# A Fourier mixing and squared-ReLU kernel: another order of its first phase and first block

## The chip, the cores and the metric

The kernel runs on one core of a Trainium2 chip. The metric is the device time of one execution in microseconds (us). The kernel before the change ran four times: 1963.38, 1964.35, 1965.85 and 1966.34 us, median 1965.1 us.

Its engines are named as in the profile: PE (TensorE, matrix products; PEld are its weight loads), DVE (VectorE), ACT (ScalarE), POOL (GpSimd) and SP (SyncE, which issues most DMAs; SPq is its queue).

## The reference

```python
def _attn_ref(x):                       # x: (8, 3008, 256)
    X = np.fft.fft(x, axis=1)
    X = np.fft.fft(X, axis=2)
    return X.real.astype(np.float32)
...
def _moe_ref(x, w_in, w_out):           # x: (24064, 256); w_in: (256, 2048); w_out: (2048, 256)
    h = x @ w_in
    r = np.maximum(h, 0.0)
    g = r * r
    return (g @ w_out).astype(np.float32)
```

The second function takes the first one's output, with batch and sequence as one axis. Everything is float32 in the kernel; the two weights arrive as float64 and are converted on the chip.

## The kernel before, in words

**Transform.** The real part of the transform over the sequence needs, for each of the 8 batches, three tables by frequency: Pt (cosine rows), Qt (sine rows) and Et (one middle column). The kernel halves the sequence again and again by symmetry. `fold(b, t)` (L340) folds one of 7 tiles of rows: three DVE steps for the P part (`f_s`, `f_sc`, `f_w`) and three for the Q part (`f_d`, `f_dc`, `f_w`). Tiles 0 to 3 are the even rows, tiles 4 to 6 the odd ones. `dft_ops(b)` (L435) gives the products: for each of P, E, Q and for even and odd frequencies (kp) a group of five operations: `even_n` (PE products over tiles 0 to 3, with cosT or sinT, and one ACT copy), `join_4` and `join_2` (DVE sums and differences), `odd_n` (PE products over tiles 4 to 6) and `join_1` (DVE, writes Pt, Et or Qt). For batch 0 the groups are numbered from 0: P 0 to 4 and 5 to 9, E 10 to 14 and 15 to 19, Q 20 to 24 and 25 to 29; number 0, 5, 10, ... is `even_n`, and so on in the order named.

**Weights.** The transform over the last axis is multiplied into w_in beforehand. `load_win(j)` (L253) loads and converts one 256-column pair of w_in (`convert`, L213: two DMAs, two DVE and three ACT operations at once; three DVE operations, L244, L246 and L247, in its `finish`); its `products` (L258) form G1 and G2 by four PE products (tile pg, L262), copied by ACT (L263), and gE by four products with a moving operand of one column (tile pe, L268) and an ACT operation. `load_wout(j)` converts one pair of w_out. Both kinds take 8 rounds (j = 0 to 7).

**Main loop.** A step (L767) is one pair j of 128-wide feature tiles for one block of 251 columns. There are 8 steps in a block, 6 blocks in a batch, 384 steps in all. `front` (L541) makes four PE products (tile ph: L551 with G1 and Pt, L552 with G2 and Qt) and six DVE operations (L554, L556, L557, twice); `combine` (L564) is ReLU and square on ACT and, outside the first block, four POOL operations; `back` (L582), two steps later (LAG = 2), adds up the output products in PSUM: eight PE products (L591) in the first block, seven (L604) afterwards, for which `sum_wout` (L278) forms sums of weights in the second block. `gather` and `store` end a block. Every float32 product is two records on PE (768 calls of L551 are 1536 records).

**Order.** The program sets the order on each engine by hand. Lines 711 to 747 write out the first phase for batch 0. The weights are a list (L683) that `next_weight` (L689) works off, up to two in a step of the first block; each call starts the next conversion and then finishes the one begun. While a batch is in the main loop, the folds and transforms of the next batch (`ahead`, L672) are let in between the halves of `front` by `between` (L754): each piece has a cost, and a pace spreads the sum over the steps. It lets in nothing in the first block, half the pace in the second, and the full pace after it.

**PSUM.** Three pools share the eight banks: psh (tag h, two buffers: ph, and pg), psd (tag d, two buffers: the transform's pd, and pe) and psm (mA, mB, mC, mD, one each; the plain `back` of the first block writes mA and mB alone).

Of the kernel before, what the change touches and what calls it, by code (L numbers as in the profile page):

```python
# [8 lines left out]
F32 = mybir.dt.float32  # L9
# [4 lines left out]
P = 128  # L14
# [67 lines left out]
def kernel(  # L82
# [12 lines left out]
    nc = tc.nc  # L95
# [7 lines left out]
    NJ = NFC // 2  # L103
# [56 lines left out]
    cosd = const.tile([P, 2, P], F32, name="cosd")  # L160
    sind = const.tile([P, 2, P - 1], F32, name="sind")
    altd = const.tile([P, 2, 1], F32, name="altd")
    cosT = const.tile([P, 2, WT], F32, name="cosT")
# [4 lines left out]
    G1 = const.tile([P, F], F32, name="G1")  # L168
    G2 = const.tile([P - 1, F], F32, name="G2")
    gE = const.tile([P, NFC], F32, name="gE")  # L170
# [17 lines left out]
    nc.vector.memset(ramp[:, 1:2], 255.0 * 2.0 ** 23)  # L188
    for dst, src in ((cosd, cos_d), (sind, sin_d), (altd, alt_d)):
        nc.scalar.dma_start(out=dst, in_=src.rearrange("(c p) m -> p c m", p=P))  # L190


# [60 lines left out]
    def load_win(j):  # L253

        w = ep.tile([P, 2, CH], F32, name="win", tag="sB" if j % 2 else "sA")
        finish = convert(parts(w, 1), pair_in(j))

        def products():  # L258
            for tab, G, n in ((cosd, G1, P), (sind, G2, P - 1)):
                ps = psh.tile([P, CH], F32, name="pg", tag="h")  # L260
                for i in range(2):
                    nc.tensor.matmul(ps[0:n], tab[:, i], w[:, i], start=i == 0, stop=i == 1)  # L262
                nc.scalar.copy(G.rearrange("p (h j f) -> j p h f", h=2, j=NJ)[j],  # L263
                               ps[0:n].rearrange("p (h f) -> p h f", h=2))
            ps = psd.tile([P, CH], F32, name="pe", tag="d")
            for h in range(2):
                for i in range(2):
                    nc.tensor.matmul(ps[:, h:h + 1], w[:, i, h * P:(h + 1) * P], altd[:, i],  # L268
                                     start=i == 0, stop=i == 1)
            nc.scalar.mul(gE[:, j::NJ], ps[:, 0:2], 0.5)  # L270

        return finish, products

    def load_wout(j):

        return convert(wout[:, j].rearrange("p h c e -> p h (c e)"), pair_out(j)), lambda: None

# [157 lines left out]
    def dft_ops(b):  # L435
# [7 lines left out]
        def group(kp, which):  # L443
# [40 lines left out]
            def odd_n():  # L484
                ps = psd.tile([P, 512], F32, name="pd", tag="d")[0:n]
                st["odd"] = ps[:, 0:n0]
# [54 lines left out]
    def front(b, k0, n, j, between):  # L541

        pt, qt, et = PQE[b]
        ks = slice(k0, k0 + n)
        g = gp.tile([P, 2, 2, CK], F32, name="g", tag="g")
        for h in range(2):
            fc = j + NJ * h
            fs = slice(fc * P, (fc + 1) * P)
            ps = psh.tile([P, 2, CH], F32, name="ph", tag="h")
            hP, hQ = ps[:, 0, 0:n], ps[:, 1, 0:n]  # L550
            nc.tensor.matmul(hP, G1[:, fs], pt[:, ks], start=True, stop=True)  # L551
            nc.tensor.matmul(hQ, G2[:, fs], qt[:, ks], start=True, stop=True)  # L552
            t = hp.tile([P, CK], F32, name="he", tag="he")[:, 0:n]
            nc.vector.scalar_tensor_tensor(out=t, in0=et[:, ks], scalar=gE[:, fc:fc + 1], in1=hP,  # L554
                                           op0=ALU.mult, op1=ALU.add)
            tt(out=g[:, h, 0, 0:n], in0=t, in1=hQ, op=ALU.add)  # L556
            tt(out=g[:, h, 1, 0:n][:, ::-1], in0=t, in1=hQ, op=ALU.subtract)  # L557
            between()
        return g
# [22 lines left out]
    def back(n, j, g, s, final):  # L582

        if j == 0:
            for nm in ("mA", "mB", "mC", "mD"):
                acc[nm] = psm.tile([P, 2, CH], F32, name=nm, tag=nm)
# [20 lines left out]
    def gather(n, plain, final):  # L607


        mA, mB, mC, mD = (acc[nm] for nm in ("mA", "mB", "mC", "mD"))  # L610
        if plain:
            c = ep.tile([P, 2, 2, CK], F32, name="c", tag="c")
            for side, m in enumerate((mA, mB)):
                nc.scalar.copy(c[:, side, :, 0:n], m[:, :, 0:n])
            return c
        sA = ep.tile([P, 2, CK], F32, name="sA", tag="sA")
        sB = ep.tile([P, 2, CK], F32, name="sB", tag="sB")
# [63 lines left out]


    weights = [lambda j=j: load_win(j) for j in range(2)]  # L683
    for j in range(NJ):
        weights.append(lambda j=j: load_wout(j))
        if j + 2 < NJ:
            weights.append(lambda j=j: load_win(j + 2))

    def next_weight():  # L689

        nonlocal begun
        (finish, products), begun = begun, weights.pop(0)() if weights else None
        finish()
        return products

    pieces = [fold(0, t) for t in range(NT)]
# [13 lines left out]

    begun = weights.pop(0)()
    for t in range(NT):
        load_x(0, t)
    load_table(cosT, cos_s, nc.sync)
    load_table(sinT, sin_s, nc.sync)
    start()
    for_p(0)
    finish, products = begun
    finish()
    products()  # L720
    for t in range(1, 4):
        for_p(t)
    groups_at(0, 5)
    for_p(4)
    for_q(0)
    for_q(1)
    groups_at(1, 2)
    for_p(5)
    groups_at(6, 7)
    for_p(6)  # L730
    groups_at(3)
    for_q(4)
    groups_at(4, 8)
    for_q(5)
    groups_at(9, 10)
    for_q(6)
    groups_at(11, 12, 13)
    begun = weights.pop(0)()
    groups_at(15)
    for_q(2)  # L740
    groups_at(14, 16, 17, 18)
    for_q(3)
    groups_at(20, 19, 25)
    products = [next_weight()]
    groups_at(21, 22, 23, 26, 27, 28)
    next_weight()
    groups_at(24, 29)
    LAG = 2
# [5 lines left out]
    def between():  # L754


        nonlocal spent
        if i < NJ or i % NJ == LAG - 1:
            return
        spent -= pace / 2 if i < 2 * NJ else pace  # L760
        while side and spent <= 0:
            t, f = side.pop(0)
            f()
            spent += t

    flight, finished = [], []
    for i in range(len(steps) + LAG + 4):  # L767
        if i < len(steps):
# [8 lines left out]
            if i % per == 0:  # L777
                assert not side
                side = ahead(b + 1) if b + 1 < B else []
                calls = 2 * (NJ - 1) * len(BLOCKS) - 6  # L780
                spent, pace = 0.0, sum(t for t, _ in side) / (calls - (0 if i else 3 * (NJ - 1)))
            g = front(b, k0, n, j, between)
            if i < NJ:
                s = combine(n, g, True)
            elif i < 2 * NJ:
                sum_wout(j)
        while finished and finished[0][0] <= i:
            store(*finished.pop(0)[1:])
        if i >= LAG and flight:
# [3 lines left out]
            if at[3] == NJ - 1:  # L793
                c_ = gather(at[2], s_ is None, final)
                finished += [(i + 2 + s, *at[:3], s, c_, final) for s in range(2)]
        for f in products:
            f()
        products = [next_weight() for _ in range(2 if 0 < i < NJ - 2 else 1 if i < NJ else 0)]
        if i < len(steps):
# [64 lines left out]
```

## Time and profile before

| what | value |
|---|---|
| runs | 1963.38, 1964.35, 1965.85, 1966.34 us; median 1965.1 |
| profiled execution, its own time | 1963.38 us |
| its span in the profile | 1961.6 us, 27513 instructions |
| PE busy | 1924.4 us (98%) |
| DVE busy | 1399.1 us (71%) |
| ACT busy | 924.8 us (47%) |
| POOL busy | 1168.8 us (60%) |
| HBM read, written | 42.39 MB, 24.68 MB |

All times in the profile count from the start of the span, so 1.8 us of the execution lie outside it. A line of the timeline gives start, duration, engine, line of the code, operation, tiles (output, then inputs), shape and count (x4: four records merged), and in brackets how long the engine had been idle and who released it. A line of the waits gives the waiting engine and line, what it waited for, the sum in us, the number of times and the longest. The duration of a matmul record runs to its modelled end and overlaps the next one; the spacing of starts is the rate. PEclk is the TensorE clock that was granted, 1.00 being full.

### The profile page before, as it was taken

The numbers are of one execution on the slowest core, as the hardware profiler recorded it, in microseconds if no ns is written. First come the engines' busy times: TensorE is split into PE (matmuls) and PEld (weight loads), VectorE is DVE, ScalarE is ACT, GpSimd is POOL, SyncE is SP. The second block draws the span as 40 slices with busy tenths as digits, with TensorE's granted clock in tenths as the row PEclk, the third lists the DMA queues.
The fourth block names the chain that finished last, engine by engine and source line by source line (L and its number), as shares of the span: only waits on it lengthen the run. The fifth ranks groups of instructions, "written<-read, shape, count | busy, mean of one in ns | idle before, by whom it ended". The sixth has DMA issues, their size and how long they took to land.

```text
span 1961.6 us, 27513 instructions
## 1 busy us (share of the span) xinstructions
PE 1924.4 (98%) x9160; PEld 1705.2 (87%) x9160; DVE 1399.1 (71%) x3434; ACT 924.8 (47%) x1076; POOL 1168.8 (60%) x1705
## 2 busy tenths in 40 slices
PE   5999999999999999999999999999999999999998
PEld 3788888888988889888998889888898888988887
DVE  7888867777677776777668776677767777655554
ACT  1654544455444444444444454444544454444443
POOL 0037745667466755666556765666756676556564
PEclk8999999999999999999999999999999999999999
DMA  6332101211021111111011200121002101100101
GB/s 189 116 44 53 27 13 40 49 27 23 13 51 41 23 26 27 41 33 35 12 35 35 46 20 12 36 52 27 20 16 52 33 11 22 27 11 11 22 11 22
DMA packets 145340, 68.88 MB, mean 35 GB/s; under 512 B 129003, under 2 KB 136110, under 8 KB 145197
## 3 DMA queue, kind: packets, MB, share of 16 engines
q1 hardware_dynamic: 144121, 66.60, 15.8%
q8 instruction: 72, 1.18, 0.3%
q10 hardware_dynamic: 1076, 0.52, 0.1%
q14 instruction: 71, 0.58, 0.1%
HBM read 42.39 MB, written 24.68 MB: 34 GB/s over the span
## 4 chain that ended last, share of the span: by engine, by line
PE 93%; DVE 4%; ACT 1%; DMA 1%; issue 0%; SPq 0%; DVEq 0%; ACTq 0%
PE ph L552 16%; PE ph L551 16%; PE mC L604 16%; PE mA L604 16%; PE mB L604 16%; PE mD L604 8%; PE pd L455 2%; PE pd L500 2%; DVE he L554 1%; DVE g L557 0%; DMA cosT<-in_cos_s_dram 0%; DVE g L556 0%; ACT g L566 0%; ACT g L567 0%; DMA xt<-in_x_dram 0%
## 5 line engine op out<-in xcount | busy, mean ns | idle before, releaser
L566 ACT ACTIVATE g<-g 128x1004 f32<-128x1004 f32 (+1 forms) x384 | 399.5, 1040 | 817.3 <-DVE g L557 439.3
L574 POOL TENSOR_TENSOR s<-g 128x251 f32<-128x251 f32 (+1 forms) x376 | 245.6, 653 | 717.6 <-ACT g L567 655.8
L554 DVE SCALAR_TENSOR_TENSOR he<-Et,gE,ph 128x251 f32<-128x251 f32 (+1 forms) x768 | 361.9, 471 | 421.9 <-PE ph L552 420.8
L551 PE MATMUL ph<-Pt,G 128*128 128x251 f32 (+1 forms) x1536 | 451.8, 375 | 4.2 <-ACT G L263 3.4
L552 PE MATMUL ph<-Qt,G 127*128 127x251 f32 (+1 forms) x1536 | 451.4, 374 | 0.4 <-DVE Qt L468 0.4
L567 ACT ACTIVATE g<-g 128x1004 f32<-128x1004 f32 (+1 forms) x384 | 399.2, 1040 | 12.1
L604 PE MATMUL mC<-s,wsum 128*128 128x251 f32 (+1 forms) x1504 | 381.4, 374 | 0.0
L604 PE MATMUL mA<-g,wout 128*128 128x251 f32 (+1 forms) x1504 | 379.8, 374 | 0.0
L556 DVE TENSOR_TENSOR g<-he,ph 128x251 f32<-128x251 f32 (+1 forms) x768 | 320.5, 417 | 54.3 <-POOL s L574 0.5
L551 PEld LDWEIGHTS ph<-Pt,G 128*128 128x128 f32 x1536 | 287.3, 189 | 42.1 <-ACT G L263 4.0
L552 PEld LDWEIGHTS ph<-Qt,G 127*128 127x128 f32 x1536 | 291.2, 190 | 36.6 <-DVE Qt L468 0.8
L604 PEld LDWEIGHTS mC<-s,wsum 128*128 128x128 f32 x1504 | 285.5, 190 | 34.6
L557 DVE TENSOR_TENSOR g<-he,ph 128x251 f32<-128x251 f32 (+1 forms) x768 | 314.4, 409 | 0.0
L604 PEld LDWEIGHTS mA<-g,wout 128*128 128x128 f32 x1504 | 282.8, 189 | 34.7 <-issue 0.6
L575 POOL TENSOR_TENSOR s<-s,g 128x251 f32<-128x251 f32 (+1 forms) x376 | 282.9, 753 | 29.5
L576 POOL TENSOR_TENSOR s<-g 128x251 f32<-128x251 f32 (+1 forms) x376 | 294.9, 784 | 0.0
L577 POOL TENSOR_TENSOR s<-g,s 128x251 f32<-128x251 f32 (+1 forms) x376 | 254.7, 677 | 0.0
L604 PE MATMUL mB<-g,wsum 128*128 128x251 f32 (+1 forms) x752 | 220.5, 374 | 0.0
L604 PE MATMUL mD<-s,wout 128*128 128x251 f32 (+1 forms) x752 | 220.3, 374 | 0.0
L604 PE MATMUL mB<-s,wout 128*128 128x251 f32 (+1 forms) x752 | 219.9, 374 | 0.0
L604 PEld LDWEIGHTS mB<-g,wsum 128*128 128x128 f32 x752 | 142.6, 190 | 17.4
L604 PEld LDWEIGHTS mD<-s,wout 128*128 128x128 f32 x752 | 141.9, 189 | 17.7
(118 smaller groups left out, 1283.0 us busy)
## 6 DMA issues: line engine op xcount, KB each, us to landing
out_dram<-os SPq DMA_DIRECT2D x376, 56.0 KB
xt<-in_x_dram SPq DMA_DIRECT2D x32, 384.0 KB
xt<-in_x_dram SPq DMA_DIRECT2D x42, 128.0 KB
Et<-e_dram SPq DMA_DIRECT2D x7, 752.5 KB
xt<-in_x_dram SPq DMA_DIRECT2D x9, 512.0 KB
out_dram<-os SPq DMA_DIRECT2D x288, 6.8 KB
raw<-in_moe_w_in_dram SPq DMA_DIRECT2D x16, 256.0 KB
raw<-in_moe_w_out_dram SPq DMA_DIRECT2D x16, 256.0 KB
```

The lines of the kernel that those rows point to most:

```text
L551: nc.tensor.matmul(hP, G1[:, fs], pt[:, ks], start=True, stop=True)
L552: nc.tensor.matmul(hQ, G2[:, fs], qt[:, ks], start=True, stop=True)
L554: nc.vector.scalar_tensor_tensor(out=t, in0=et[:, ks], scalar=gE[:, fc:fc + 1], in1=hP, op0=ALU.mult, op1=ALU.add)
L556: tt(out=g[:, h, 0, 0:n], in0=t, in1=hQ, op=ALU.add)
L557: tt(out=g[:, h, 1, 0:n][:, ::-1], in0=t, in1=hQ, op=ALU.subtract)
L566: act(v, v, AF.Relu)
L567: act(v, v, AF.Square)
L574: gt(out=s1, in0=g21, in1=g22, op=ALU.add)
L575: gt(out=s2, in0=s1, in1=g11, op=ALU.subtract)
L576: gt(out=s3, in0=g11, in1=g21, op=ALU.subtract)
L577: gt(out=s4, in0=g12, in1=s2, op=ALU.subtract)
L604: nc.tensor.matmul(acc[nm][:, i, 0:n], w, v[:, 0:n], start=j == 0 and i == 0, stop=j == NJ - 1, skip_group_check=True)
```

## The change

The first x tiles are loaded ahead of the first weights. The first phase has a new order: the P parts of all tiles come ahead of the first join, the Q parts of the odd rows (tiles 4 to 6) ahead of those of tiles 1 to 3. `odd_n` of batch 0 takes its PSUM buffer from psh in place of psd. `awake(n)` issues n float32 products of the 128x128 identity with itself into a tile that nothing reads; 96 stand ahead of everything else on PE, 20 more behind the first weight products. The alternating column altd becomes column 127 of the sine table, so that G2 has 128 rows, the last of which holds what pe held; `for_e` takes it out with two one-column products and a DVE multiplication in place of four products and an ACT operation. pg takes mC and mD in place of psh. The weights have an order of their own (`weights`, `leftover`): in each step of the first block, behind `front`, the products of the pair j = i + 1, the start of one w_out, the finish of the w_in of i + 2, the start of that of i + 3; behind `back`, the finish of w_out and `for_e`. Before the main loop no w_out is converted. `between` lets in nothing in the second block, and the pace is the sum over the steps that are left.

```diff
@@ -158,15 +158,14 @@
         nc.sync.dma_start(out=xt[b, t][0:rows], in_=x[b, r0:r0 + step * (rows - 1) + 1:step])
     cosd = const.tile([P, 2, P], F32, name="cosd")
-    sind = const.tile([P, 2, P - 1], F32, name="sind")
-    altd = const.tile([P, 2, 1], F32, name="altd")
+    sind = const.tile([P, 2, P], F32, name="sind")
     cosT = const.tile([P, 2, WT], F32, name="cosT")
     sinT = const.tile([P, 2, WT], F32, name="sinT")
     wout = const.tile([P, NJ, 2, 2, H], F32, name="wout")
     wsum = const.tile([P, 3, NJ, H], F32, name="wsum")
     ident = const.tile([P, P], F32, name="ident")
     G1 = const.tile([P, F], F32, name="G1")
-    G2 = const.tile([P - 1, F], F32, name="G2")
+    G2 = const.tile([P, F], F32, name="G2")
     gE = const.tile([P, NFC], F32, name="gE")
     def load_table(tab, src, engine):
@@ -186,8 +185,15 @@
     ramp = const.tile([P, 2], F32, name="ramp")
     nc.vector.memset(ramp[:, 0:1], 1151.0)
     nc.vector.memset(ramp[:, 1:2], 255.0 * 2.0 ** 23)
-    for dst, src in ((cosd, cos_d), (sind, sin_d), (altd, alt_d)):
+    for dst, src in ((cosd, cos_d), (sind[:, :, 0:P - 1], sin_d), (sind[:, :, P - 1:], alt_d)):
         nc.scalar.dma_start(out=dst, in_=src.rearrange("(c p) m -> p c m", p=P))
+    filled = psm.tile([P, CH], F32, name="filled", tag="mB")
+    def awake(n):
+        for _ in range(n):
+            nc.tensor.matmul(filled[:, 0:P], ident, ident, start=True, stop=True)
     def pair_in(j):
@@ -256,24 +262,27 @@
         finish = convert(parts(w, 1), pair_in(j))
         def products():
-            for tab, G, n in ((cosd, G1, P), (sind, G2, P - 1)):
-                ps = psh.tile([P, CH], F32, name="pg", tag="h")
+            for tab, G, nm in ((cosd, G1, "mC"), (sind, G2, "mD")):
+                pg = psm.tile([P, CH], F32, name="pg", tag=nm)
                 for i in range(2):
-                    nc.tensor.matmul(ps[0:n], tab[:, i], w[:, i], start=i == 0, stop=i == 1)
+                    nc.tensor.matmul(pg, tab[:, i], w[:, i], start=i == 0, stop=i == 1)
                 nc.scalar.copy(G.rearrange("p (h j f) -> j p h f", h=2, j=NJ)[j],
-                               ps[0:n].rearrange("p (h f) -> p h f", h=2))
+                               pg.rearrange("p (h f) -> p h f", h=2))
+        def for_e():
             ps = psd.tile([P, CH], F32, name="pe", tag="d")
             for h in range(2):
-                for i in range(2):
-                    nc.tensor.matmul(ps[:, h:h + 1], w[:, i, h * P:(h + 1) * P], altd[:, i],
-                                     start=i == 0, stop=i == 1)
-            nc.scalar.mul(gE[:, j::NJ], ps[:, 0:2], 0.5)
-        return finish, products
+                fc = j + NJ * h
+                nc.tensor.matmul(ps[:, h:h + 1], G2[:, fc * P:(fc + 1) * P], ident[:, P - 1:], start=True, stop=True)
+            return lambda: nc.vector.tensor_scalar_mul(gE[:, j::NJ], ps[:, 0:2], 0.5)
+        return finish, products, for_e
     def load_wout(j):
-        return convert(wout[:, j].rearrange("p h c e -> p h (c e)"), pair_out(j)), lambda: None
+        return convert(wout[:, j].rearrange("p h c e -> p h (c e)"), pair_out(j))
     def sum_wout(j):
@@ -482,7 +491,9 @@
                 both(st["c"][:, 0:n1], st["c"][:, n1:n0], a, ps[:, 2 * n2:2 * n2 + n1])
             def odd_n():
-                ps = psd.tile([P, 512], F32, name="pd", tag="d")[0:n]
+                pool, tag = (psh, "h") if b == 0 else (psd, "d")
+                ps = pool.tile([P, 512], F32, name="pd", tag=tag)[0:n]
                 st["odd"] = ps[:, 0:n0]
                 if not b:
                     return product(ps[:, 0:n0], 3)
@@ -549,7 +560,7 @@
             ps = psh.tile([P, 2, CH], F32, name="ph", tag="h")
             hP, hQ = ps[:, 0, 0:n], ps[:, 1, 0:n]
             nc.tensor.matmul(hP, G1[:, fs], pt[:, ks], start=True, stop=True)
-            nc.tensor.matmul(hQ, G2[:, fs], qt[:, ks], start=True, stop=True)
+            nc.tensor.matmul(hQ, G2[0:P - 1, fs], qt[:, ks], start=True, stop=True)
             t = hp.tile([P, CK], F32, name="he", tag="he")[:, 0:n]
             nc.vector.scalar_tensor_tensor(out=t, in0=et[:, ks], scalar=gE[:, fc:fc + 1], in1=hP,
                                            op0=ALU.mult, op1=ALU.add)
@@ -582,7 +593,7 @@
     def back(n, j, g, s, final):
         if j == 0:
-            for nm in ("mA", "mB", "mC", "mD"):
+            for nm in ("mA", "mB") if s is None else ("mA", "mB", "mC", "mD"):
                 acc[nm] = psm.tile([P, 2, CH], F32, name=nm, tag=nm)
         if s is None:
             for c in range(2):
@@ -607,12 +618,13 @@
     def gather(n, plain, final):
-        mA, mB, mC, mD = (acc[nm] for nm in ("mA", "mB", "mC", "mD"))
+        mA, mB = acc["mA"], acc["mB"]
         if plain:
             c = ep.tile([P, 2, 2, CK], F32, name="c", tag="c")
             for side, m in enumerate((mA, mB)):
                 nc.scalar.copy(c[:, side, :, 0:n], m[:, :, 0:n])
             return c
+        mC, mD = acc["mC"], acc["mD"]
         sA = ep.tile([P, 2, CK], F32, name="sA", tag="sA")
         sB = ep.tile([P, 2, CK], F32, name="sB", tag="sB")
         u = ep.tile([P, 3, CK], F32, name="u", tag="u")
@@ -680,19 +692,6 @@
                 + groups + [(0.0, lambda: load_e(1))])
-    weights = [lambda j=j: load_win(j) for j in range(2)]
-    for j in range(NJ):
-        weights.append(lambda j=j: load_wout(j))
-        if j + 2 < NJ:
-            weights.append(lambda j=j: load_win(j + 2))
-    def next_weight():
-        nonlocal begun
-        (finish, products), begun = begun, weights.pop(0)() if weights else None
-        finish()
-        return products
     pieces = [fold(0, t) for t in range(NT)]
     start, *groups = [f for _, f in dft_ops(0)]
@@ -708,43 +707,50 @@
         for i in which:
             groups[i]()
-    begun = weights.pop(0)()
-    for t in range(NT):
+    def rounded(j):
+        win[j][0]()
+    start()
+    awake(96)
+    load_x(0, 0)
+    load_x(0, 1)
+    for_p(0)
+    for_q(0)
+    for_p(1)
+    win = [load_win(0)]
+    for t in range(2, NT):
         load_x(0, t)
     load_table(cosT, cos_s, nc.sync)
     load_table(sinT, sin_s, nc.sync)
-    start()
-    for_p(0)
-    finish, products = begun
-    finish()
-    products()
-    for t in range(1, 4):
-        for_p(t)
+    for_p(2)
+    rounded(0)
+    win[0][1]()
+    awake(20)
+    for_p(3)
     groups_at(0, 5)
     for_p(4)
-    for_q(0)
+    for_p(5)
+    for_p(6)
+    groups_at(3, 8, 1, 2)
+    for_q(4)
+    groups_at(6, 7)
+    for_q(5)
+    groups_at(10, 15, 4)
+    for_q(6)
+    groups_at(9, 13, 18, 11, 12, 16, 17)
     for_q(1)
-    groups_at(1, 2)
-    for_p(5)
-    groups_at(6, 7)
-    for_p(6)
-    groups_at(3)
-    for_q(4)
-    groups_at(4, 8)
-    for_q(5)
-    groups_at(9, 10)
-    for_q(6)
-    groups_at(11, 12, 13)
-    begun = weights.pop(0)()
-    groups_at(15)
+    groups_at(14, 23)
+    win.append(load_win(1))
+    groups_at(19, 28)
+    copy_e = win[0][2]()
     for_q(2)
-    groups_at(14, 16, 17, 18)
     for_q(3)
-    groups_at(20, 19, 25)
-    products = [next_weight()]
-    groups_at(21, 22, 23, 26, 27, 28)
-    next_weight()
-    groups_at(24, 29)
+    groups_at(20, 25)
+    copy_e()
+    win.append(load_win(2))
+    rounded(1)
+    groups_at(21, 22, 24, 26, 27, 29)
     LAG = 2
     BLOCKS = [(k0, min(CK, NKT - k0)) for k0 in range(0, NKT, CK)]
     steps = [(b, k0, n, j) for b in range(B) for k0, n in BLOCKS for j in range(NJ)]
@@ -755,13 +761,34 @@
         nonlocal spent
-        if i < NJ or i % NJ == LAG - 1:
+        if i < 2 * NJ or i % NJ == LAG - 1:
             return
-        spent -= pace / 2 if i < 2 * NJ else pace
+        spent -= pace
         while side and spent <= 0:
             t, f = side.pop(0)
             f()
             spent += t
+    late = []
+    def weights():
+        if i + 1 < NJ:
+            win[i + 1][1]()
+        now = i - 1 if i < NJ - 1 else i
+        if now >= 0:
+            late.append(load_wout(now))
+        if i + 2 < NJ:
+            rounded(i + 2)
+        if i + 3 < NJ:
+            win.append(load_win(i + 3))
+        elif i == NJ - 2:
+            late.append(load_wout(i))
+    def leftover():
+        while late:
+            late.pop(0)()
     flight, finished = [], []
     for i in range(len(steps) + LAG + 4):
@@ -777,12 +804,14 @@
             if i % per == 0:
                 assert not side
                 side = ahead(b + 1) if b + 1 < B else []
-                calls = 2 * (NJ - 1) * len(BLOCKS) - 6
-                spent, pace = 0.0, sum(t for t, _ in side) / (calls - (0 if i else 3 * (NJ - 1)))
+                calls = 2 * (NJ - 1) * (len(BLOCKS) - (0 if i else 2)) - 6
+                spent, pace = 0.0, sum(t for t, _ in side) / calls
             g = front(b, k0, n, j, between)
             if i < NJ:
+                weights()
                 s = combine(n, g, True)
             elif i < 2 * NJ:
+                leftover()
                 sum_wout(j)
         while finished and finished[0][0] <= i:
             store(*finished.pop(0)[1:])
@@ -793,9 +822,9 @@
             if at[3] == NJ - 1:
                 c_ = gather(at[2], s_ is None, final)
                 finished += [(i + 2 + s, *at[:3], s, c_, final) for s in range(2)]
-        for f in products:
-            f()
-        products = [next_weight() for _ in range(2 if 0 < i < NJ - 2 else 1 if i < NJ else 0)]
+        if i + 1 < NJ:
+            late.append(win[i + 1][2]())
+            leftover()
         if i < len(steps):
             flight.append(((b, k0, n, j), g, s if i < NJ else combine(n, g, False)))
```

## Prediction

> **What bounds the kernel now.** I read the page first: PE is busy 98% of the span and carries 93% of the chain that ended last. Then the waits of PE, by stretches, ask where it is not busy.
>
> ```profile
> PE   5999999999999999999999999999999999999998
> ...
> PE 93%; DVE 4%; ACT 1%; DMA 1%; issue 0%; SPq 0%; DVEq 0%; ACTq 0%
> ```
>
> ```profile
> engine line waited for: us in total, times, longest us
> PE ph L551 <- DVE g L557: 0.8, 1, 0.8
> ```
>
> The second fence holds all waits of PE from 110 to 300 us; from there to the end there is one more of 0.5 us. So the work from the second block on is a block of PE time that nothing else can shorten. What an edit can win is the time at which PE gets into it, about 109 us. The windows by stage show what leads there (the columns are length, then busy time and count of PE, PEld, DVE, ACT, POOL, then clock and DMA):
>
> ```profile
> 5.30:22.00 16.70, 7.09 (x23) 5.61 (x24) 13.37 (x33) 2.92 (x6) 0.00 (x0) 0.93 0.85 212
> 22.00:54.30 32.30, 23.80 (x83) 15.40 (x84) 27.82 (x76) 7.23 (x15) 0.00 (x0) 0.88 0.61 180
> 54.30:109.00 54.70, 50.14 (x250) 42.41 (x250) 47.70 (x102) 40.63 (x70) 0.00 (x0) 1.00 0.32 97
> 200.00:240.00 40.00, 40.00 (x190) 35.60 (x189) 35.33 (x84) 21.92 (x30) 27.64 (x42) 1.00 0.11 23
> ```
>
> Both early stages are filled by DVE to 86 and 87%, and PE has slack. The first phase ends with the first DVE operation of the main loop (L554) at 54.33 us, the first block's seventh interval with that of step 7 at 109.03. The sum has three parts: the first phase, the first block, and what comes later.
>
> **The dummies, the largest new item.** PE works in order, so `awake(96)`, the first weight products, `awake(20)` and the first transform products follow one another. Rows for a small product:
>
> ```profile
> 12.10 2.07 PE L262 MATMUL pg<-win,cosd 128*128 128x256 f32 x4 [12.10 <-DVE win L247]
> 13.97 1.91 PE L262 MATMUL pg<-win,sind 128*127 128x256 f32 x4
> 15.67 1.16 PE L268 MATMUL pe<-altd,win 128*128 128x1 f32 x8
> 19.53 0.71 PE L455 MATMUL pd<-cosT,w 95*128 95x95 f32 x2 [2.70 <-DMA cosT<-in_cos_s_dram]
> ```
>
> Single starts, read in narrow windows: at full clock records of one to 95 columns follow each other by 0.111 us, and 256 columns by 0.213, hence 0.107 for 128; the larger one counts. With two records a dummy is 0.222 us. While the array is slow (L262 here, 0.427 a record, twice 0.213) it is 0.427. Slow stretches last 4.0 us (12.1 to 16.1) to 6.6 (19.5 to 26.1, granted clock 0.50), so they cost the dummies 1.9 to 3.2 us. The identity is ready at 1.3 us (POOL). `awake(96)` ends at 1.4 + 96 x 0.222 + 1.9 to 3.2 = 24.6 to 25.9; I take 25.0, since PE starts there as it does at 12.1. The four products of the first w_in take 8 x 0.213 = 1.7 (26.7), `awake(20)` 4.4 (31.1), the first `even_n` 4 x 0.111 + 4 x 0.16 = 1.1, its latency and copy 0.5: the first join can start at **32.7**. In the profile it starts at 23.06.
>
> **When DVE wants it.** In the new order DVE has seven P parts (1.66 each, from 11.96 to 13.62), one Q part (1.58), and the first w_in (2 x 0.34 + 2.0 = 2.7): 15.9 us. It starts when x tile 0 lands: 8.4 now, behind two DMAs of weights (issues 0.75 and 1.50); with its issue at 0.75 instead of 2.13 and 256 KB fewer ahead (1.1 us at 227 GB/s), 5.5 to 7. It waits about 1.2 us for tile 2. So DVE is at the first join at 22.5 to 24, and waits 9 to 10 us. SP issues the same DMAs; the tables stay behind the x tiles, so the start of cosT on PE (19.53) is no later than now, and it is covered by the dummies.
>
> **First phase, rest of it.** Behind the first join: six groups of joins (0.98 + 0.91 = 1.89, 11.3), six Q parts (9.5), the second w_in (2.7), the start of a third (0.7), a gE copy (0.15): 24.3 us, and 0.3 to the first L554. PE's own work there (each `odd_n` 6 x 0.32 = 1.9, each `even_n` 1.1) stays ahead of DVE, as the odd products no longer share two buffers with the even ones: I walked the order, and each join finds its product done. So the first phase ends at 32.7 + 24.3 + 0.3 = 57.3: **3.0 later** (2 to 4.5). One w_out (2.7) has moved out of this phase into the first block.
>
> **The clock inside it.** In that walk PE has nothing from 43.2 to 45.8, ahead of the odd rows of Q. Gaps of 2.7 us (16.8 to 19.5) and 3.0 (37.3 to 40.3) were followed by a clock of 0.50, a gap of 2.3 (46.4 to 48.7) was not. If this one is, `odd_n` and the gE copy behind it come 1.8 us late. The gap lies between the rows: **0.9** of 0 to 1.8. [...]
>
> **First block.** One step now, from the start of its front on PE to the next:
>
> ```profile
> 70.52 1.02 PE L262 MATMUL pg<-win,cosd 128*128 128x256 f32 x4
> 71.40 1.13 PE L262 MATMUL pg<-win,sind 128*127 128x256 f32 x4
> 72.37 0.95 PE L268 MATMUL pe<-altd,win 128*128 128x1 f32 x8
> 73.81 0.69 PE L551 MATMUL ph<-Pt,G 128*128 128x251 f32 x2 [0.49 <-ACT G L263]
> ```
>
> ```profile
> 67.00 0.69 DVE L244 SCALAR_TENSOR_TENSOR fd<-raw,fd 128x512 uint32<-128x512 uint32 x1 [0.75 <-ACT fd L237]
> ```
>
> 65.31 to 73.81 is 8.50 us: 1.7 of front, 3.4 of back, 1.7 of pg with 0.26 of waiting for the buffer, 1.1 of pe, 0.5 of waiting for ACT, as pg and ph share psh. With pg in mC and mD both waits go; `for_e` halves pe to 0.5: PE needs 7.3. DVE needs 2.32 (front), two conversions of 2.68 and about 0.15 for gE that ACT did: **7.85**. Its wait of 0.75 at L244 goes, as w_in's ACT work is begun a step earlier. ACT needs 6.8 (0.6 + 3 x 2.06). So DVE sets the step. DVE from the first L554 to that of step 7: step 0 5.15 (no w_out), step 1 8.0, steps 2 to 4 7.85 each, step 5 7.15, step 6 (two w_out, ACT's six conversions in a row) 8.3: 52.15, against 54.7 now. And PE is further ahead then: its back of step 5 waits only for that w_out, 2.15 before DVE begins step 7; now it begins 0.5 behind it. From there PE has work without a gap, by my walk through steps 7 to 10. The first block gives 2.55 + 2.65 = **5.2 less** (3 to 6); the w_out moved into it is in this sum.
>
> **Later.** The 0.8 us wait (158 us, behind folds of 1.7 us in the second block) goes, with 6.8 us of folds that fall on blocks 3 to 6. There the pace rises from 1/57 to 1/50 of the sum, 14%. DVE is busy 88% there (200 to 240), of it some 31% side work: 92 to 93%. The second block now, with 0.8 lost in 37 us at 93%, is the nearest row, so 0 to 2.5 lost over three blocks; I take 0.8. **Net 0** (-0.8 to +1.7).
>
> **Sum (A):** +3.0 + 0.9 - 5.2 + 0 = -1.3 on the profiled 1963.4: 1962.1. The runs' median is 1.7 above that execution, so **1963.8**. Its bounds, 1960 to 1967.5, come from adding the parts' ends about half way.
>
> **Rivals.**
> B, the dummies are half as long. The trace shows products with the identity as one record each:
>
> ```profile
> 1952.36 1.35 PE L653 MATMUL po<-ident,c 128*125 128x128 f32 x7 [0.50 <-DVE c L631]
> ```
>
> Eight transposes are eight records here, 0.107 apart. Were a dummy one record, `awake(96)` would end at about 14 us, within the wait for w_in, and the 20 at 19.3, as cosT lands (19.5). The first join would start at 22.9, the phase end at 47.5 (6.8 earlier) and the time be 1965.1 - 6.8 - 5.2 + 0.9 = **1954**. For it: both counts would fit the gaps they stand in. Against it: a transpose is its own mode, and every plain product here is two records, even of one column. [...] Anything that makes DVE's wait at the first join short ends here.
>
> C, slower: the first block does not get shorter. The ACT chain is the mechanism, its place the two ReLU and square operations (1.04 each) that now stand behind six conversions in ACT's order, so that a finish of w_out waits for L241 in every step. If the steps stay at 8.5 the 5.2 is lost: 1965.1 + 3.0 + 0.9 = **1969**. It decides from steps of 8.35 on. Against it: ACT's 6.8 in 7.85.
>
> D, slower: the clock stays low under the dummies. 96 x 0.427 = 41 us instead of 23.6, all 17 of it late: **1981**. It loses to A from about 13 us of further half clock. Against it: no slow stretch is over 6.6 us.
>
> **How the numbers follow.** A measurement of this kernel can tell about 0.2% (3.9 us) from no change. A has 0.46 (0.07 faster, 0.36 same, 0.03 slower), B 0.32 (faster), C 0.15 (0.05 same, 0.10 slower), D 0.07 (slower). Faster 0.39, same 0.41, slower 0.20. The range reaches from 1952.5 (most of B) to 1969 (A and half of C); D and the ends of B and C, 2 in 10, are left out.
>
> **What would show it.** The first row of the changed PE timeline: dummies to 25 us (A) or 14 (B); two records for each or one. DVE's wait at the first join: 9 us or under 1. The first L554 at 57 to 58. Steps of 7.85 in the first block, DVE without L244 waits, no PE wait for ACT's L263. No clock of 0.50 behind 26 us but at one gap. PE waits of under 3 us from 110 on. A first L554 ahead of 52, or steps over 8.3, would make A wrong.

## The result and the profile after the change

The changed kernel takes 1967.81 us (median of 40 runs, 1966.59 to 1969.02), the kernel before 1964.15 us (60 runs, 1959.85 to 1966.69). The ratio is 1.0019, 95% interval 1.0014 to 1.0023: slower by 0.19%, where 0.07% faster was forecast. The profiled execution took 1966.59 us with a span of 1964.8 us, against 1963.38 and 1961.6 before, so 3.2 us of difference can be followed through the traces.

The page of the changed kernel, PE's row of the 40 slices and the chain that ended last by engine:

```profile
PE   9899999999999999999999999999999999999998
...
PE 93%; DVE 5%; ACT 0%; issue 0%; DMA 0%; SPq 0%; DVEq 0%; POOL 0%; POOLq 0%; ACTq 0%
```

The first slice rose from 5 to 9. Those are the dummies, whose results nothing reads. DVE has one more per cent of the chain. PE is still the bound of nearly the whole span, and the time is still decided by when PE gets into the main loop and how often it stalls there.

The timeline of the changed kernel, PE and DVE in the first 45 us (columns: start, duration, engine, line, operation, tiles, shape, count, idle time before and its releaser):

```profile
1.37 24.36 PE L196 MATMUL filled<-ident 128*128 128x128 f32 x192 [1.37 <-POOL fs L212]
...
25.56 1.03 PE L268 MATMUL pg<-win,cosd 128*128 128x256 f32 x4
...
27.29 4.63 PE L196 MATMUL filled<-ident 128*128 128x128 f32 x40
...
31.75 12.39 PE L464 MATMUL pd<-cosT,w 95*128 95x95 f32 x56
...
33.31 0.25 DVE L477 TENSOR_TENSOR db<-da,pd 128x95 f32<-128x95 f32 x1 [12.23 <-ACT da L472]
```

96 dummies are 192 records, 20 are 40. The last row is the first join. DVE has stood idle for 12.23 us when it starts; PE does useful work only from 25.56 us, and the first transform product comes at 31.75.

Windows of the changed kernel (length, then busy time and count of PE, PEld, DVE, ACT, POOL, then clock, DMA share, GB/s):

```profile
22.00:40.00 18.00, 18.00 (x127) 16.26 (x126) 6.48 (x19) 1.46 (x5) 0.00 (x0) 1.00 0.63 176
...
58.00:110.00 52.00, 48.63 (x226) 41.00 (x224) 48.26 (x109) 39.35 (x62) 0.00 (x0) 0.97 0.32 102
...
128.00:164.00 36.00, 36.00 (x171) 31.83 (x170) 30.68 (x79) 17.11 (x18) 22.36 (x34) 1.00 0.40 28
164.00:200.00 36.00, 35.35 (x165) 30.45 (x164) 33.41 (x71) 15.84 (x17) 23.94 (x33) 1.00 0.24 59
200.00:240.00 40.00, 38.76 (x179) 33.31 (x178) 35.77 (x81) 19.84 (x25) 26.39 (x38) 1.00 0.17 43
```

DVE falls to 36% (6.48 of 18.00) in the stretch that the dummies block, and rises to 93% in the first block (48.26 of 52.00; 87% before). From 164 to 240 us PE loses 1.9 us, where before it lost nothing: from 200 to 240 us its 40.00 of 40.00 became 38.76. From 164 to 200 us the kernel before has

```profile
164.00:200.00 36.00, 36.00 (x171) 31.81 (x170) 31.48 (x72) 16.66 (x17) 27.05 (x36) 1.00 0.27 66
```

The waits of PE in the changed kernel, from 125 to 300 us (engine, tile and line, what it waited for, sum in us, times, longest):

```profile
PE ph L562 <- DVE g L568: 1.7, 3, 1.1
```

One wait of 0.8 became three of 1.7 in all. That is less than what was lost. A row's duration runs 0.16 us past the start of the next one (0.59 at a spacing of 0.43), and a stall shorter than that does not show as idle time. The starts do show it. I therefore set the two traces against each other by the start of each step's front on PE (before L551, after L562), and at the start of the loop by the first DVE operation (L554, L565):

| from ... to | later than before, us | gained or lost on the way | forecast |
|---|---|---|---|
| start ... first DVE operation of the loop (54.33; 58.63) | +4.30 | +4.30 | +3.9 |
| ... front of step 9 (118.11; 118.92) | +0.80 | -3.50 | -5.2 |
| ... front of step 19 (166.72; 166.22) | -0.50 | -1.30 | -0.8 |
| ... front of step 35 (241.61; 244.68) | +3.07 | **+3.57** | +0.8 |
| ... end of the span (1961.6; 1964.8) | +3.2 | +0.1 | 0 |

At step 19 the changed kernel was ahead. It lost its lead, and 3 us more, between 166 and 245 us.

The main loss has a place. DVE of the changed kernel around it:

```profile
223.73 1.43 DVE L439 SCALAR_TENSOR_TENSOR w<-w,turn,f 128x256 f32<-128x256 f32 x2 [1.40 <-ACT f L425]
225.09 0.47 DVE L565 SCALAR_TENSOR_TENSOR he<-Et,gE,ph 128x251 f32<-128x251 f32 x1
...
225.92 0.41 DVE L568 TENSOR_TENSOR g<-he,ph 128x251 f32<-128x251 f32 x1
```

and PE, the second half of step 31's front:

```profile
226.39 0.69 PE L562 MATMUL ph<-Pt,G 128*128 128x251 f32 x2 [1.09 <-DVE g L568]
```

L439 is a piece of the next batch's fold. It was let in before ACT had made its input (L425 starts at 222.44, behind the square of a step, and lasts 1.26). It stands between the halves of step 30's front. The second half (L565 at 225.09) comes behind it in DVE's order and starts only after the 1.40 us of waiting and the 1.43 of L439, though its products had ended by 221.5. So the buffer of ph comes free late, step 31's second half waits on PE, and at step 32 the lag behind the trace of before has grown by 1.35 us. No such wait of DVE for ACT's f is in the trace of before from 160 to 300 us. The other 2.2 us of the 3.57 are six delays of 0.2 to 0.6 us at steps 20 to 34 (less one gain of 0.1). Nearly every step there has fold pieces between the halves of its front; what made each of the six was not followed.

### The profile page after: what moved, and what is told of

Its sections match the earlier page's. It is cut to its first block, busy times and chain, and to the rows that moved or that the text cites. A ratio compares the mean times of both kernels' runs of the same rounds, so it can differ in the third digit from the quotient of the medians.

```text
span 1964.8 us, 27915 instructions
## 1 busy us (share of the span) xinstructions
PE 1944.4 (99%) x9360; PEld 1726.8 (88%) x9360; DVE 1405.2 (72%) x3442; ACT 925.0 (47%) x1068; POOL 1168.8 (59%) x1705
## 4 chain that ended last, share of the span: by engine, by line
PE 93%; DVE 5%; ACT 0%; issue 0%; DMA 0%; SPq 0%; DVEq 0%; POOL 0%; POOLq 0%; ACTq 0%
PE ph L562 16%; PE ph L563 16%; PE mC L615 16%; PE mA L615 16%; PE mB L615 16%; PE mD L615 8%; PE pd L464 2%; PE pd L511 2%; PE filled L196 1%; DVE he L565 1%; DVE w L395 1%; DVE g L568 0%; DVE g L567 0%; DVE m L252 0%; DVE fd L250 0%
## 5 line engine op out<-in xcount | busy, mean ns | idle before, releaser
L565 DVE SCALAR_TENSOR_TENSOR he<-Et,gE,ph 128x251 f32<-128x251 f32 (+1 forms) x768 | 362.0, 471 | 416.1 <-PE ph L563 414.1
L562 PE MATMUL ph<-Pt,G 128*128 128x251 f32 (+1 forms) x1536 | 453.3, 376 | 4.7 <-DVE Qt L479 2.7
L567 DVE TENSOR_TENSOR g<-he,ph 128x251 f32<-128x251 f32 (+1 forms) x768 | 320.5, 417 | 55.1 <-POOL s L585 1.0
L562 PEld LDWEIGHTS ph<-Pt,G 128*128 128x128 f32 x1536 | 287.4, 189 | 43.7 <-DVE g L568 5.9
L568 DVE TENSOR_TENSOR g<-he,ph 128x251 f32<-128x251 f32 (+1 forms) x768 | 314.4, 409 | 0.0
```

## The experiments

All ratios are to the kernel before, run on the same chip. Differences "by medians" to the changed kernel are taken across chips, on which the kernel before has medians of 1963.0 to 1964.8 us; where they differ from the traces, the traces are the closer measure.

**The pace of the folds alone, on the kernel before.**

```diff
-        if i < NJ or i % NJ == LAG - 1:
+        if i < 2 * NJ or i % NJ == LAG - 1:
...
-        spent -= pace / 2 if i < 2 * NJ else pace
+        spent -= pace
...
-                calls = 2 * (NJ - 1) * len(BLOCKS) - 6
-                spent, pace = 0.0, sum(t for t, _ in side) / (calls - (0 if i else 3 * (NJ - 1)))
+                calls = 2 * (NJ - 1) * (len(BLOCKS) - (0 if i else 2)) - 6
+                spent, pace = 0.0, sum(t for t, _ in side) / calls
```

> The kernel before with the fold pace of the changed kernel alone (nothing let in during the second block, the sum spread over the steps that are left). Theory 1 (the pace is a cost of its own: in the aligned traces the changed kernel loses 3.6 us against before between steps 19 and 35 and wins 0.9 at step 18): about +2.6 us against before, front of step 19 earlier by 0.9, that of step 36 later by 2 to 3. Rival (the losses there come from the changed kernel's later start and its late conversions, not from the pace): within 0.5 us of before.

Measured: 1966.3 us against 1963.99, ratio 1.0015 (1.0006 to 1.0023), so 2.3 us slower. Its windows:

```profile
164.00:200.00 36.00, 35.61 (x167) 30.97 (x166) 33.18 (x72) 16.34 (x17) 25.05 (x34) 1.00 0.24 58
200.00:240.00 40.00, 38.77 (x180) 33.30 (x179) 35.69 (x82) 19.81 (x26) 26.40 (x38) 1.00 0.18 43
```

PE loses time in the same two windows as in the changed kernel. By the starts it is 0.48 us ahead of before at steps 18 and 19 and 2.56 behind at steps 34 and 35, and that stays, so 3.04 are lost on the same steps. Of the changed kernel's 3.57, 0.53 came at step 24; this run does not show that delay, and its cause stays open. The row of the long stall is there as well:

```profile
223.22 1.43 DVE L430 SCALAR_TENSOR_TENSOR w<-w,turn,f 128x256 f32<-128x256 f32 x2 [1.40 <-ACT f L416]
```

Its first DVE operation of the loop already came 0.8 us later than in the trace of before, ahead of anything that the edit touches. So the pace by itself is worth 2.5 - 0.8 = +1.7 us by the traces. Nothing else of the change is needed to make this loss. About +2.6 was expected, and the place is as expected; but 0.8 of the total is not the pace's.

**The old pace in the changed kernel.** The same edit the other way round.

> The changed kernel with the pace of before (half in the second block). Theory 1: the loss between steps 19 and 35 goes, 3 to 4 us less than the changed kernel, and up to 1 us comes back in the second block: about 1965. Rival (the second block of the changed kernel has late conversions and cannot take folds): 1967 to 1969, the loss moves to steps 8 to 17.

Measured: 1966.3 us, ratio 1.0009 (1.0000 to 1.0018); 1.5 us better than the changed kernel by medians. Windows of this kernel:

```profile
128.00:164.00 36.00, 35.24 (x164) 30.42 (x164) 33.63 (x84) 16.09 (x18) 21.68 (x30) 1.00 0.42 32
...
200.00:240.00 40.00, 40.00 (x190) 35.61 (x189) 34.74 (x82) 22.94 (x32) 27.77 (x41) 1.00 0.11 23
```

The loss after 200 us is gone and the 0.76 us before 164 are back. Against the trace of before it is 2.3 us late at step 10 and 2.4 at the end: nothing more is lost behind the first block. 3 to 4 us less than the changed kernel were expected; by the traces it is 0.9. One reason is that its loop began 0.8 us later than that of the changed kernel, ahead of anything that the edit touches. The waits of DVE from 30 to 61 us show why:

```profile
DVE gE L279 <- PE pe L277: 1.5, 1, 1.5
```

PE stands idle for 2.27 us ahead of the odd rows of Q, as it does in the changed kernel (2.26). Here the clock was 0.50 behind that gap (46.29 to 49.70 us) and the gE copy came late; there it stayed at 1.00 and the gE copy did not wait.

**No dummies.** Both calls of `awake` are left out.

```diff
-    awake(96)
...
-    awake(20)
```

> The changed kernel without its 116 dummies. Theory 2 (DVE's wait of 12 us at the first join is the dummies' doing, and the phase behind it is DVE work): first join at 23 to 25 in place of 33.3, first DVE operation of the main loop 8 to 10 us earlier than 58.6, time about 1958 to 1960, with a low clock in the first products costing 1 to 2 of the 10. Rival (the dummies earn their time by the clock, or tables and weights land too late for an earlier join): less than 3 us gained.

Measured: 1958.23 us, ratio 0.9969 (0.9956 to 0.9981), 9.6 less than the changed kernel. DVE of this kernel at the first join:

```profile
21.41 0.25 DVE L476 TENSOR_TENSOR db<-da,pd 128x95 f32<-128x95 f32 x1 [0.33 <-ACT da L471]
```

DVE's wait of 12.23 us is down to 0.33, the join comes 11.9 earlier and the loop's first DVE operation (48.89) 9.7 earlier. The clock is at 0.50 from 23 to 29 us now, and the first phase gives 2.2 of those 11.9 back (DVE waits 1.4 for products in it, where it waited for none). The span ends 9.5 earlier. Without the dummies the changed kernel is faster than the one before: the new order of the first phase then gains 54.33 - 48.89 = 5.4 us.

**Short dummies.** 48 and 12 in place of 96 and 20, to end about when w_in and cosT arrive.

```diff
-    awake(96)
+    awake(48)
...
-    awake(20)
+    awake(12)
```

> The changed kernel with 48 and 12 dummies in place of 96 and 20. At 0.222 us each 56 fewer are 12.4 us of PE. Theory 2: first join at 22 to 23.5, nothing lost to the clock, time about 1957 to 1958, 1 to 2 us below the kernel without dummies. Rival (the clock is not worth keeping up, since PE has slack here): the same as without dummies within 0.7 us. Rival (tables or weights land too late): less than 3 us gained.

Measured: 1957.56 us, ratio 0.9967 (0.9954 to 0.9979): the same as without dummies (by trace the span is 0.4 longer, by medians 0.7 shorter). The first join starts at 22.53, 1.1 later than without dummies: the 48 end before w_in is ready (PE waits 0.78 us for it), but the 12 do not end in time, and the first transform product follows them at 19.69, where it started at 18.33 without them. The clock fell at 26 us nevertheless (0.55 from 26 to 28 us, 0.60 from 28 to 30). What the short dummies still cost at the join, the clock gave back up to 0.4 us; they neither gain nor lose anything that the runs can tell from zero.

**The PSUM banks alone, on the kernel before.** pg in mC and mD, as in the change, with mC and mD taken by the plain `back` no more.

```diff
-                ps = psh.tile([P, CH], F32, name="pg", tag="h")
+                ps = psm.tile([P, CH], F32, name="pg", tag=nm)
```

> The kernel before with one part of the change: pg takes the banks mC and mD in place of psh, and the plain back takes mA and mB alone. Theory of the prediction (the step of 8.5 us has 0.75 of PE waits for the shared buffers): the waits go and seven steps lose 0.5 to 0.75 each, 3.5 to 5 us less than before. Theory 3 (the step is a ring of ACT and DVE: ReLU, square, copies of G, two conversions on ACT, then three DVE operations of w_in and the six of front; PE's waits lie beside it): PE's wait for ACT's copy goes, steps stay at 8.4 to 8.5, time within 1 us of before.

Measured: 1963.6 us against 1964.81, ratio 0.9997 (0.9988 to 1.0006): no change. The steps stay at 8.50. The waits of PE in the first block, in the kernel before:

```profile
PE ph L551 <- ACT G L263: 3.4, 7, 0.5
PE pg L262 <- DVE g L557: 1.1, 2, 0.6
```

and in this run:

```profile
PE ph L551 <- ACT G L263: 4.7, 6, 1.6
```

and of DVE in this run (3.8, 5, 0.8 before):

```profile
DVE fd L244 <- ACT fd L237: 3.7, 5, 0.8
```

PE no longer waits for a buffer ahead of pg, so it waits longer for ACT behind it. The chain of waits of the kernel before shows the ring that sets 8.50: g L566 (1.05), g L567 (1.04), two copies of G (0.54), L236 (0.62), L237 (0.73), then on DVE L244, L246, L247 and the front up to L557 (some 4.4), and again L566. No PSUM buffer is in it. My conclusion then was that the banks do nothing and that the order of the conversions made the whole gain. The next run shows that this was too much.

**The banks taken back in the changed kernel.** pg in psh again, all else as in the change.

```diff
-            for tab, G, nm in ((cosd, G1, "mC"), (sind, G2, "mD")):
-                pg = psm.tile([P, CH], F32, name="pg", tag=nm)
+            for tab, G in ((cosd, G1), (sind, G2)):
+                pg = psh.tile([P, CH], F32, name="pg", tag="h")
```

> The changed kernel with one edit taken back: pg, the products of w_in, takes its buffer from psh again, which it shares with ph. Theory, after the run on the banks alone: what shortened the first block is the order of the conversions (the ACT work of a w_in is begun a step earlier, so that DVE does not wait at L250), not the banks; PE waits more, but DVE still sets the step. Then the steps 1 to 4 stay at 7.9 to 8.1 us and the time stays within 1.0 of the changed kernel's 1967.8: 1967 to 1969. Rival, the forecast's own reason: both were needed, and with pg back in psh the front waits for ACT's copies of G. Then the steps go back to 8.3 to 8.5, four to six steps lose 0.4 to 0.6 each, and the time is 1970 to 1971.

Measured: 1973.31 us against 1963.04, ratio 1.0051 (1.0038 to 1.0065): 5.5 us slower than the changed kernel by medians, 6.4 by the traces. The theory of the run before fell, the rival holds, though with another wait than it named. PE of this kernel in one step:

```profile
81.71 0.67 PE L562 MATMUL ph<-Pt,G 128*128 128x251 f32 x2
...
84.15 1.13 PE L268 MATMUL pg<-win,cosd 128*128 128x256 f32 x4 [0.49 <-DVE g L568]
...
90.04 0.67 PE L562 MATMUL ph<-Pt,G 128*128 128x251 f32 x2
```

Steps are 8.33 (81.71 to 90.04). In the changed order pg comes ahead of `back`. With psh it can start only when DVE has read both halves of ph (L568), and `back` (3.4), pe and the next front stand behind it in PE's order: a second ring, of 8.33. By the starts 1.1 us is lost in the first phase and 5.3 in the first block up to step 10; from there the distance is constant at 6.42. The 1.1 is not the banks': it is the clock behind the gap of 2.27 us again (0.50 from 46.99 to 50.40, and 1.5 of waiting for the gE copy, as in the changed kernel with the old pace). Of the 5.3, by the first DVE operation of each step, 2.4 lie in steps 2 to 5, which take 8.33 each; 2.0 in steps 6 and 7, not followed; and 0.7 in step 0, in which half clock lasted longer (to 64.06). So the old order has a ring of 8.50 through ACT, the new order with the old banks one of 8.33 through psh, and only the two together let DVE set the step, at 7.93.

**No dummies and the old pace.** The two costs taken out together.

> The changed kernel without dummies and with the pace of before. If the two costs are separate and add up: 1958.2 without dummies, less 1.5 to 2 for the pace, 1956 to 1957; front of step 36 on PE behind that of step 8 by as much as in before. If the earlier start leaves the folds short of DVE again: 1958.

Measured: 1955.19 us, ratio 0.9952 (0.9939 to 0.9966). The gains add up, and a little over: 12.6 by medians against 9.6 + 1.5. By the starts it is 9.25 ahead of the changed kernel at step 8 and 11.2 at step 45.

**A few dummies at another place.** As the last, with ten of them where PE has nothing to do ahead of the first front.

```diff
     groups_at(20, 25)
+    awake(10)
     copy_e()
```

> The same with ten dummies at another place: behind the even products of Q, in the gap of 2.7 us ahead of the first front, after which the clock fell to half in the changed kernel (fronts and G products of steps 0 and 1 at 0.43 a record, first step 6.1 us in place of 5.15). Theory 4 (that spell of half clock is on the path): first DVE operation of the main loop 0.5 to 0.8 earlier, step 0 1 us shorter, 1 to 1.8 us less than without them: about 1955. Rival (DVE sets steps 0 and 1, PE has slack): the same within 0.5 us.

Measured: 1954.29 us, ratio 0.9948 (0.9936 to 0.9961), the fastest version: 13.5 us less than the changed kernel and about 10 less than before. Against the last run it is 0.82 ahead from step 4 to 20, and 0.26 from step 21 on: most of what is won early is lost at the next stall, and the intervals of the two overlap. Nor is the lead the dummies' doing: in the profiled execution of the last run DVE waited 2.1 us for the DMA of a w_in ahead of the loop, here 0.4. The clock fell here too (0.50 from 48.39 to 51.80), and step 0 did not get 1 us shorter, as the theory had it: it took 6.32 us, against 5.75 in the last run.

**The 20 dummies alone.** The changed kernel without `awake(20)`.

```diff
-    awake(20)
```

> The changed kernel without the 20 dummies behind the first weight products, the 96 kept. Theory 2 says that each dummy delays the first join by its 0.222 us one to one as long as DVE waits: first join at 28.7 to 28.9 in place of 33.3, 4.4 to 4.7 us less than the changed kernel, about 1963.2. Rival (what follows the first join has slack of its own): less than 2 us.

Measured: 1961.42 us, ratio 0.9986 (0.9978 to 0.9995). By the starts it is 5.2 ahead of the changed kernel at step 0 and 5.12 to 5.15 all the way to the end. The first join comes at 28.09, 5.22 earlier. Of this, 4.46 us are the 20 dummies (27.29 to 31.75 in the changed kernel); the other 0.76 is that the 96 ended earlier in this execution, whose clock rose at 5.4 us and not at 7.0. What the 20 take passes one to one into the total.

## Why the prediction was wrong, step by step

**The dummies: right.** Two records each; the products behind the 96 began at 25.56 (25.0 forecast), the 20 took 4.63 (4.4), the first join came at 33.31 (32.7). DVE waited 12.2 and not 9 to 10, for it was ready at 21.1 and not at 22.5 to 24. That did not matter, since PE and not DVE decides the join. Rivals B (one record) and D (clock low throughout) are out.

**The rest of the first phase: right.** 33.31 to 57.79 is 24.5, where 24.3 was worked out.

**The clock: near in the first phase by luck, and 1.0 missing behind it.** The gap that I priced (PE idle for 2.26 us at 44 to 46) was followed by full clock in the profiled execution and cost nothing there; in two other runs the same gap was followed by half clock and cost 1.5. So 0 to 1.8 was a fair range, and it is the execution that decides. The next gap, 2.74 us ahead of the first front, was followed by half clock (0.50 from 54.75 to 61.58 us). DVE waits 0.84 us at its first L565, 0.54 more than the 0.3 that I had for it, and this stands by chance where the 0.9 stood. Step 0 lasts 6.14 where 5.15 was forecast (DVE waits 0.42 and 0.54 us for products in it), and for this 1.0 us, which stands in the first block's row of the table, I had nothing. That it is the clock, eight executions with the new order agree: the longer half clock lasts behind the loop's first DVE operation, the longer is step 0, in the same order throughout, from 5.75 us with 2.2 us left (no dummies, old pace) over 6.14 with 2.95 (the changed kernel) to 6.99 with 4.7 (no dummies). The slow stretch of the kernel before that I read as ending at 26.1 us ends at 26.34.

**The first block: right in mechanism, too good by 1.7.** DVE sets the step: 7.93 in steps 1 to 4 (8.0 and 7.85 forecast), 7.14 in step 5, 8.45 in step 6 (8.3). DVE of the changed kernel in one of them:

```profile
80.63 0.47 DVE L565 SCALAR_TENSOR_TENSOR he<-Et,gE,ph 128x251 f32<-128x251 f32 x1
...
87.68 0.69 DVE L253 SCALAR_TENSOR_TENSOR wout<-m,fd 128x512 f32<-128x512 f32 x1
88.29 0.15 DVE L279 TENSOR_SCALAR gE<-pe 128x2 f32<-128x2 f32 x1
88.56 0.48 DVE L565 SCALAR_TENSOR_TENSOR he<-Et,gE,ph 128x251 f32<-128x251 f32 x1
```

The stretch holds the front, two conversions and the gE copy, with no wait for ACT in it. Its 7.93 is DVE's own work in a row (busy 7.64 us, the rest gaps of a few hundredths between operations). Of the missing 1.7 us, 1.0 is the clock in step 0. Another 0.3 is the sum of the steps 1 to 6 (47.3 where 47.0 was worked out), and 0.3 is lost between the fronts of steps 8 and 9 (+0.50 and +0.80). The reason that I gave, shared banks, was one of two: the banks alone do nothing, and without them the new order loses 4.6 to 5.3 us in the first block. Rival C (steps stay at 8.5) is out.

**The step that failed is the term called "Later".** It read that 0 to 2.5 us would be lost over three blocks, "I take 0.8. Net 0". The wait at 158 us went, as said, and steps 9 to 19 gave even 1.3. But 3.57 were lost between steps 19 and 35, above the upper end that I gave. The two runs on the pace place it: the new pace alone makes the kernel before lose 3.04 on those steps, and with the old pace none of the loss is left in the changed kernel. The mean load of DVE that I worked out was right (92 to 93% forecast; 93 and 89% in the two windows). What I read from it was not. PE runs ahead by two buffers of ph, so what stalls it is the pieces that fall into one step, and not the mean over 36 or 40 us: the longest loss, 1.35, is one fold operation that waited 1.40 us for ACT with a front queued behind it. The nearest row that I used, one wait of 0.8 in the second block, could not show this, since DVE never waited for ACT's f there. Only this 1.35 was followed to its cause; for the smaller delays it is shown that the pace makes most of them, not how.

With 3.6 in place of 0.8, 3.5 in place of 5.2, 4.3 in place of 3.9 and 1.3 in place of 0.8 my own sum gives +4.3 - 3.5 - 1.3 + 3.6 = +3.1, which is what the traces show (+3.2). Against the forecast of -1.3 that is 4.4 us off: 2.3 of it are "Later" (2.3 net in place of 0), 1.7 the first block, 0.4 the first phase. Either of the two larger ones alone turns the sign: with the forecast's other terms "Later" as measured gives +1.0, the first block as measured +0.4.

## What to carry to other kernels

Filler work that stands ahead of real work in an engine's order is on the path as soon as it ends later than the real work could start: here 24.4 and 4.6 us of dummies held the first join up by 11.9, and what the full clock that they bought gave back was at most 2.4 (without them the end came 9.5 earlier). When side work is packed more densely, do not price it by the mean load of its engine, but look step by step for a piece that can wait for another engine with the main work queued behind it (here one wait of 1.40 us for ACT, behind which 1.35 us were lost). And when an edit takes a resource out of a loop, work out the next ring as well: here the new banks alone gained nothing, the new order with the old banks reached 8.33, and only the pair brought the step to 7.93.

## What the runs showed of the hardware

In these traces gaps of PE of nearly the same length were followed by different granted clocks. Windows of the changed kernel around its gap of 2.74 us (53.10 to 55.84), with the clock behind the five busy times:

```profile
54.00:56.00 2.00, 0.16 (x1) 0.16 (x1) 1.93 (x7) 1.27 (x2) 0.00 (x0) 0.69 0.73 220
56.00:58.00 2.00, 1.66 (x4) 0.87 (x5) 1.73 (x5) 0.00 (x0) 0.00 (x0) 0.50 0.12 42
```

The clock was 0.50 from 54.75 to 61.58 us. A gap of 2.26 us in the same execution (44.15 to 46.41) left it at 1.00. In the changed kernel with the old pace a gap of 2.27 us at the same place was followed by 0.50 (46.29 to 49.70). In the fastest version the ten dummies cut the gap to two of 0.83 and 0.86 us, and the clock fell all the same (0.50 from 48.39 to 51.80). Windows of that version:

```profile
46.00:48.00 2.00, 1.05 (x4) 0.59 (x4) 1.93 (x7) 0.00 (x0) 0.00 (x0) 1.00 0.23 82
48.00:50.00 2.00, 2.00 (x7) 1.62 (x6) 1.34 (x5) 0.00 (x0) 0.00 (x0) 0.60 0.00 0
```

There PE was busy 1.05 of 2 us just before the fall. So the length of the gap alone does not tell these cases apart: 2.26 us was followed by full clock, 2.27 by half, and the pair of 0.83 and 0.86 us by half as well. What does decide was not shown.
